# A planned order for five engines, drawn up again with other assumptions on instruction pages

## The chip, the cores and the metric

The kernel runs on one NeuronCore of one Trainium2 chip. The core has five engines with a queue of instructions each: TensorE (PE: matmuls from SBUF into PSUM), VectorE (DVE), ScalarE (ACT), GpSimd (POOL) and SyncE (SP, which here only issues transfers). Transfers run on 16 DMA engines. The metric is device time in microseconds (us) of one execution, 278.59 before (median of 3 runs, 278.31 to 279.34).

## The reference

`x` is 4 batches of 12800 rows of 128, `inducing` is 32 rows of 128. First two attention steps, then a gated layer:

```
def mab(q, kv):
    s = scale * (q @ kv.transpose(0, 2, 1))
    s = s - s.max(-1, keepdims=True)
    a = np.exp(s)
    a /= a.sum(-1, keepdims=True) + 1e-09
    return a @ kv
h = mab(I, x)                 # 32 x 128 for each batch: sums over all 12800 rows
x = mab(x, h)                 # every row attends to the 32 rows of h
gate_pre += conv_w[k][None, None, :] * xp[:, k:k + S, :]     # k = 0..4, causal
gate = 1.0 / (1.0 + np.exp(-gate_pre))
val = x @ w_val
return (gate * val @ w_out)
```

The 32 weights `a` of a row go straight into the gate and value matmuls, with `h` folded into the weights.

## The kernel before

A batch is cut into four strips of 3200 rows that lie on four groups of 32 partitions, and a strip into 7 or 8 chunks of up to 480 columns (`SIZES`). In all there are 29 chunks. Each chunk goes through these stages, whose names are those of the table `ORDER`:

- `s1`: scores of the inducing rows against the chunk (L476), copied out with their maximum by DVE (L484).
- `x` (first batch only): transposes of the chunk on PE (L451), evicted by ACT or DVE, in place of a second load.
- `gm`: maximum over a group of chunks (L497 on POOL, L505 on PE, L512 on DVE).
- `h`: exponentials (ACT, L522), transposes (DVE, L527) and the sums over the rows on PE (L542), added up by DVE (H, L552 and L554).
- `u`: normalisation of a batch's sums (ACT and POOL, then L591 and L592 on PE); `w`: gate and value weights from it (L610); `W`: their transposes on PE (L666), two halves, copied out by ACT or DVE (L676, L674); `po`: scaling of the output weights (L694).
- `s2`: second attention of a chunk: scores (L740), then a chain of softmax steps over DVE, POOL and ACT up to the tiles `P1` and `P2` (L813, L820).
- `r k`: r block k: gate matmuls of chunk k (L834) and, put in at two places of it, value matmuls of chunk k-1 (L843). ACT takes the tanh (L893), DVE multiplies (L903), ACT and POOL split the product into two halves (L916, L921).
- `o k r`: output of strip r of chunk k, three matmuls (L944 to L946; L937 for the last chunk), evicted by DVE if its number is in `OUTV`, else by ACT (L959, L961), and stored.
- `z`: fillers, matmuls on zeros (L998) that do nothing but keep PE going; eight more (L987) stand at the very start.

PE gets its work in the order of `ORDER`, word for word. For the other engines a planner, `lay`, sets the order: it keeps a clock for each engine, takes the next step whose inputs are there, and of several the one that PE needs first, where `URGE` shifts each kind of step. Its durations are constants of the source. Loads of `xt` and `xk` are issued on SP up to the first r block and on ACT from then on (`sp`, L409 and L423), in the place that the planner gives them; a load into a buffer that is still read waits at the head of its queue. Stores are issued on SP, four of the end on ACT. Eight semaphores go round among all transfers, so a transfer also waits until the last one on its semaphore has landed.

PE uses its array in three kinds of tiling: `full` (x, u, w, o, z), `strips` of 32 columns (s1, s2, gm, h, W, po) and `rows` of 32 (r). A change of kind has a price in the plan (`SWITCH`).

The plan also keeps account of PE's instructions. They come in pages of 256. The plan has a page asked for when PE is 0.68 of a page into the one before the last (`ASK`), and lets it arrive after a time that depends on the loads then under way, `bus - t`, at most `LINE`, and on `FETCH`; where PE comes to the page earlier, the plan lets it wait:

```
asked.append(t + min(max(bus - t, 0.0), LINE) + FETCH)
```

These are numbers of the plan; nothing of them is sent to the chip but the orders that come out.

Of the kernel before, what the change touches and what calls it, by code (L numbers as in the profile page):

```python
# [45 lines left out]
PAGE, ASK, NEED, LINE, FETCH = 256, 0.68, 1.8, 3.8, 2.5  # L46
# [8 lines left out]
class Plan:  # L55
# [87 lines left out]
    def lay(self, deps, succ, topo, nominal):  # L143
# [30 lines left out]
        while len(seq) < n:  # L174
# [21 lines left out]
            if e == "PE":  # L196
# [7 lines left out]
                while told > PAGE * (len(asked) + ASK):  # L204
                    t = start + (PAGE * (len(asked) + ASK) - begun) / w * work
                    asked.append(t + min(max(bus - t, 0.0), LINE) + FETCH)
# [44 lines left out]
def tile_kernel(ctx: ExitStack, tc: tile.TileContext, xt, xk, indT_in, w64, out):  # L251
# [827 lines left out]
    "tile_kernel.f_ind": 88.5,  # L1079
    "tile_kernel.f_zero": 58,  # L1080
    "tile_kernel.f_const": 124.5,
    "tile_kernel.f_mask": 39,
    "tile_kernel.warm_up": -3,
    "idle.f": 301.5,
    "load_xt.f": -120.5,
    "s1.f": -326.5,
    "s1.g": -126,
    "make_xk.ones": 310,
    "make_xk.tp": 180,
    "make_xk.ev": 114,  # L1090
    "make_xk.<lambda>": -72.5,
    "gmax.f0": 489,
    "gmax.f1": -64.5,
    "gmax.f2": 52,
    "e1.f": 26,
    "e1.tr": 172,
    "h.f": -105.5,
    "h.acc": 342.5,
    "tile_kernel.f_wload": 46.5,
    "weights.start": -12.5,  # L1100
    "weights.<lambda>": 78.5,
    "weights.cmax": 313,
    "load_xk.f": -235,
    "prep.f0": 155,
    "prep.<lambda>": -308,
    "prep.f1": -97,
    "prep.f2": 12.5,
    "prep.f3": -151.5,
    "prep.f4": 186,
    "s2.f": -222.5,  # L1110
    "s2.tin": 120.5,
    "s2.mx": 65,
    "s2.sub": -115.5,
    "s2.ex": 101.5,
    "s2.sm": -96.5,
    "s2.sa": -18.5,
    "s2.rz": 34.5,
    "s2.nm": 43.5,
    "s2.tout": 70.5,
    "s2.hi": -298,  # L1120
    "s2.lo": -152,
    "prep2.f4": 26,
    "prep2.g0": 79.5,
# [86 lines left out]
```

## Time and profile before

| | before |
|---|---|
| median of the runs, us | 278.59 (278.31 to 279.34) |
| profiled execution, us | 278.39 |
| its span, us | 276.3 |
| PE busy, us | 267.6 |
| DVE, ACT, POOL busy, us | 230.7, 197.1, 207.5 |
| moved by DMA | 75.41 MB, mean 273 GB/s |

The span is the stretch that the profiler sees; the profiled execution has 2.1 us around it. Busy time of PE counts a matmul from its start to a modelled end, and matmuls overlap in the pipeline: a PE that is busy all the time isn't at its peak, and the distance of two starts tells what one costs. The four matmuls of a group of strips or rows run beside each other, so their starts lie a few ns apart. An f32 matmul is two records, a transpose one. Where one engine waits for another, the views name the instruction that ended the wait; "issue" is time in which PE waited for nothing that the profile shows.

### The profile page before, as it was taken

To read this page: it belongs to the slowest core of one execution; us is meant where nothing else is said; L and a number is where in the kernel's file an instruction comes from. 1 tells how busy PE (TensorE), PEld (TensorE's weight loads), DVE (VectorE), ACT (ScalarE), POOL (GpSimd) and SP (SyncE) were. 2 spreads that over 40 slices of the span, in tenths; PEclk is the share of its full clock that TensorE was granted. 3 is DMA by queue.
4 is the path that set the end of the run, shared out by engine and by line. 5 is a ranking of instruction groups with operands and counts; after the bars stand their busy time and mean duration, and the time that the engine had idled before them with its cause. 6 is when DMAs were issued, how large, how long until landed. Compare 5 with 4: busy or idle time off the path is not lost.

```text
span 276.3 us, 10032 instructions
## 1 busy us (share of the span) xinstructions
PE 267.6 (97%) x4118; PEld 140.5 (51%) x4118; DVE 230.7 (83%) x542; ACT 197.1 (71%) x298; POOL 207.5 (75%) x236
## 2 busy tenths in 40 slices
PE   8999899999999999999999999999999999999983
PEld 2567546446644564475444564574444445444541
DVE  0378799999889999888889999989889998785851
ACT  2366368668848885887668778876668888787773
POOL 2000378799578999985876999998689999998650
PEclk9999999999999999999999999999999999999999
DMA  7999999997999979999949897422533125325538
GB/s 278 422 420 411 414 412 384 372 368 256 346 369 393 310 274 329 385 362 362 391 170 293 255 400 293 179 99 97 187 120 114 70 103 214 135 108 209 186 125 302
DMA packets 35373, 75.41 MB, mean 273 GB/s; under 512 B 2816, under 2 KB 26752, under 8 KB 35328
## 3 DMA queue, kind: packets, MB, share of 16 engines
q1 hardware_dynamic: 19120, 42.03, 39.7%
q10 hardware_dynamic: 16208, 32.75, 33.7%
q8 instruction: 32, 0.52, 0.8%
q14 instruction: 13, 0.11, 0.1%
HBM read 48.56 MB, written 26.21 MB: 271 GB/s over the span
## 4 chain that ended last, share of the span: by engine, by line
PE 91%; DVE 4%; ACT 2%; POOL 1%; issue 1%; POOLq 0%; ACTq 0%
PE g L834 30%; PE a L944 9%; PE a L740 8%; PE a L476 8%; PE a L946 8%; PE a L945 8%; PE a L542 7%; PE a L843 6%; PE g L998 2%; PE g L451 2%; PE a L987 1%; PE a L666 1%; DVE ss L484 1%; PE a L937 1%; DVE et L527 1%
## 5 line engine op out<-in xcount | busy, mean ns | idle before, releaser
L921 POOL TENSOR_TENSOR gl<-tg,gh 128x960 f16<-128x960 f32 (+4 forms) x56 | 104.8, 1881 | 16.1 <-PE a L946 10.2
L834 PE MATMUL g<-P,W 32*128 32x480 f16 (+4 forms) x1740 | 102.8, 345 | 0.1
L903 DVE SCALAR_TENSOR_TENSOR tg<-tg,a 128x480 f32<-128x480 f32 (+4 forms) x116 | 65.4, 604 | 10.1 <-PE a L843 8.5
L916 ACT CAST gh<-tg 128x960 f16<-128x960 f32 (+4 forms) x56 | 51.9, 929 | 29.3 <-DVE tg L903 28.8
L834 PEld LDWEIGHTS <-W 32*128 32x128 f16 x1740 | 50.6, 92 | 40.9 <-issue 10.0
L893 ACT ACTIVATE tg<-g,gsc 128x960 f32<-128x960 f32 (+4 forms) x58 | 55.5, 990 | 3.3 <-PE g L834 2.5
L843 PE MATMUL a<-P,W 32*128 32x480 f16 (+4 forms) x348 | 41.5, 344 | 0.2
L959 DVE TENSOR_SCALAR os<-a,osc 128x480 f32<-128x480 f32 (+4 forms) x62 | 40.0, 670 | 1.8 <-PE a L946 1.3
L944 PE MATMUL a<-gh,wo 128*128 128x480 f16 (+4 forms) x112 | 39.6, 354 | 0.7 <-DVE tg L903 0.7
L945 PE MATMUL a<-gh,wo 128*128 128x480 f16 (+4 forms) x112 | 39.3, 351 | 0.0
L946 PE MATMUL a<-gl,wo 128*128 128x480 f16 (+4 forms) x112 | 39.3, 351 | 0.0
L961 ACT ACTIVATE os<-a,osc 128x480 f32<-128x480 f32 (+4 forms) x46 | 28.1, 629 | 7.9 <-PE a L946 7.8
L820 POOL TENSOR_TENSOR P<-pt,P 128x480 f16<-128x480 f32 (+4 forms) x29 | 30.0, 1036 | 2.0 <-ACT P L813 1.0
L802 POOL TENSOR_TENSOR e<-e,z 128x480 f32<-128x480 f32 (+4 forms) x29 | 27.2, 938 | 4.6 <-DVE z L795 2.7
L757 POOL TENSOR_TENSOR e<-e,m 128x480 f32<-128x480 f32 (+4 forms) x29 | 27.0, 937 | 2.6 <-DVE m L751 2.2
L542 PE MATMUL a<-xk,et 128*32 128x129 f32 x800 | 27.9, 274 | 1.1 <-DVE H L554 0.6
L542 PEld LDWEIGHTS a<-xk,et 128*32 128x32 f32 x800 | 24.4, 110 | 6.5 <-issue 2.6
L740 PE MATMUL a<-xt,hT 128*32 128x480 f32 (+4 forms) x232 | 27.7, 543 | 0.0
L476 PE MATMUL a<-xt,indT 128*32 128x480 f32 (+4 forms) x232 | 26.6, 538 | 0.0
L484 DVE TENSOR_SCALAR_CACHE_REDUCE ss<-a 128x480 f32<-128x480 f32 (+4 forms) x29 | 17.3, 605 | 10.2 <-PE a L476 9.1
L763 ACT ACTIVATE e<-e 128x480 f32<-128x480 f32 (+4 forms) x29 | 16.6, 571 | 6.9 <-POOL e L757 6.7
L944 PEld LDWEIGHTS <-wo 128*128 128x128 f16 x112 | 11.2, 100 | 19.8 <-issue 10.4
(111 smaller groups left out, 322.9 us busy)
## 6 DMA issues: line engine op xcount, KB each, us to landing
out_dram<-os SPq DMA_DIRECT2D x52, 240.0 KB, 2.5
xt<-in_xt_dram ACTq DMA_DIRECT2D x11, 960.0 KB, 8.1
out_dram<-os SPq DMA_DIRECT2D x44, 224.0 KB, 3.4
xk<-in_xk_dram ACTq DMA_DIRECT2D x9, 967.5 KB, 9.1
xk<-in_xk_dram ACTq DMA_DIRECT2D x7, 903.0 KB, 7.4
xt<-in_xt_dram SPq DMA_DIRECT2D x6, 960.0 KB, 9.7
xt<-in_xt_dram ACTq DMA_DIRECT2D x5, 896.0 KB, 6.9
xk<-in_xk_dram SPq DMA_DIRECT2D x4, 903.0 KB, 12.8
```

The costliest lines, as they stand in the source:

```text
L476: T.matmul(s[32 * r:32 * r + 32, :n], c_["indT"], x[:, o:o + n // 32, r, :], start=True, stop=True)
L542: T.matmul(t[32 * s:32 * s + 32, :P + 1], st["et", b, c][:, 32 * i:32 * i + 32], st["xk", b, q][:, m + i, :], start=j < R, stop=j >= len(b ...
L740: T.matmul(s[32 * r:32 * r + 32, :n], st["hT", b], x[:, m:m + nb, r, :], start=True, stop=True)
L834: T.matmul(st[f"g{r // 2}", b, c][:, r % 2, :n], st["W", b][q, w, k, :], st[("P1", "P2")[e]][q, o:o + n], start=u == 0, stop=u == len(taps ...
L843: T.matmul(st["a", "v", b, c, r][:, :n], st["W", b][q, w, TAPS, :], st[("P1", "P2")[e]][q, o:o + n], start=u == 0, stop=u == 2)
L893: S.activation(t[:, :, :n], st[f"g{p}", b, c][:, :, :n], AF.Tanh, scale=st["gsc", b])
L903: V.scalar_tensor_tensor(t, t, 1.0, st["a", "v", b, c, r][:, :n], ALU.add, ALU.mult)
L916: S.copy(sb(pw, g1, [P, 2, CW], F16)[:, :, :n], st[tg][:, :, :n])
L921: G.tensor_tensor(sb(pw, g2, [P, 2, CW], F16)[:, :, :n], st[tg][:, :, :n], st[g1][:, :, :n], ALU.subtract)
L944: T.matmul(t, w[:, 0], st[g1][:, q, :n], start=True, stop=False)
L945: T.matmul(t, w[:, 1], st[g1][:, q, :n], start=False, stop=False)
L946: T.matmul(t, w[:, 0], st[g2][:, q, :n], start=False, stop=True)
```

## The change

Two lines of the planner's account of pages are changed, and everything that a search chooses is chosen anew under them: `ORDER` (with the places of the value matmuls in the r blocks), `URGE` and `OUTV`. The work itself is the same: the same matmuls and tiles, 24 matmuls on zeros, the same bytes in and out.

```
-PAGE, ASK, NEED, LINE, FETCH = 256, 0.68, 1.8, 3.8, 2.5
+PAGE, ASK, NEED, LINE, FETCH = 256, 0.68, 1.8, 4.0, 2.5
...
-                    asked.append(t + min(max(bus - t, 0.0), LINE) + FETCH)
+                    asked.append(t + (max(bus - t, 0.0) + 0.3 if bus - t < 0.8 and not 36.0 < t < 56.0 else LINE if t < 40.0 else LINE + 0.8) + FETCH)
...
 ORDER = [
-    ('z', 10, 2), ('z', 4, 1), ('z', 11, 2), ('s1', 0, 0), ('s1', 0, 2), ('x', 0, 2), ('x', 0, 0), ('s1', 0, 1),
...
+    ('s1', 0, 0), ('x', 0, 0), ('z', 11, 2), ('z', 4, 1), ('s1', 0, 1), ('x', 0, 1), ('s1', 0, 2), ('x', 0, 2),
...
-    "rblock.f": -517.5,
+    "rblock.f": -618,
...
-    1, 3, 4, 7, 8, 9, 11, 12, 14, 15, 20, 21, 23, 24, 25, 28, 31, 32, 34, 35, 36, 37, 39, 42, 43, 44, 45, 48, 52,
+    0, 1, 2, 3, 4, 6, 7, 11, 12, 13, 14, 20, 21, 22, 24, 25, 26, 32, 33, 34, 35, 36, 37, 38, 42, 44, 45, 49, 50, 53,
```

In the plan a page now comes 0.3 + 2.5 after the loads under way if these end within 0.8 us (and not between 36 and 56 us), else always the full 4.0 + 2.5 or, from 40 us on, 4.8 + 2.5 after it is asked for. Outside that stretch it was at most 3.8 + 2.5 and less where the loads ended sooner. `OUTV` holds 67 outputs instead of 66. Of changes of kind `ORDER` holds 116 instead of 109: 15 instead of 12 up to the first `u`, 27 instead of 21 up to `r 1`.

PE just after the eight matmuls at the start, before: two groups of fillers, then the scores of chunk 0 and of chunk 2.

```order
22 L998 MATMUL g_142<-zero 128x512
23 L998 LDWEIGHTS zero
24 L998 MATMUL g_144<-zero 128x512
25 L998 LDWEIGHTS zero
26 L998 MATMUL g_144<-zero 128x512
27 L476 MATMUL a<-xt,indT 32x128 x4
28 L476 MATMUL a<-xt,indT 32x480 x4
29 L451 MATMUL g_160<-identf,xt 128x128 x8
```

The same place of PE after (L476 32x128 is chunk 0, 32x320 chunk 1, 32x480 chunk 2; L451 are their transposes):

```order
17 L476 MATMUL a<-xt,indT 32x128 x4
18 L451 MATMUL g_144<-identf,xt 128x128 x4
19 L998 LDWEIGHTS zero
20 L998 MATMUL g_152<-zero 128x512
21 L998 LDWEIGHTS zero
22 L998 MATMUL g_152<-zero 128x512
23 L998 LDWEIGHTS zero
24 L998 MATMUL g_156<-zero 128x512
25 L476 MATMUL a<-xt,indT 32x320 x4
26 L451 MATMUL g_163<-identf,xt 128x128 x8
```

Scores and transposes of chunk 0 now stand ahead of the fillers, of which three stand here instead of five, and chunk 1 comes before chunk 2.

PE behind r block 1, before: one chunk's second scores, then the first three groups of sums of the second batch (L542, 14 instructions each), then an output.

```order
446 L834 MATMUL g_831<-P_115,W 128x320
447 L740 MATMUL a<-xt,hT 32x480 x4
448 L542 MATMUL a<-xk,et 32x129 x42
449 L944 LDWEIGHTS wo
450 L944 MATMUL a<-gh,wo 128x128
451 L945 LDWEIGHTS wo
452 L945 MATMUL a<-gh,wo 128x128
```

The same place of PE after:

```order
449 L834 MATMUL g_830<-P_115,W 128x320
450 L542 MATMUL a<-xk,et 32x129 x14
451 L740 MATMUL a<-xt,hT 32x480 x4
452 L542 MATMUL a<-xk,et 32x129 x14
453 L476 MATMUL a<-xt,indT 32x448 x4
454 L834 LDWEIGHTS W
455 L834 MATMUL g_1000<-P_115,W 128x480
```

The second scores have moved between the first two groups of sums, the third group has left the place, and the first scores of a chunk of the second batch (L476) stand in front of r block 2.

ACT around the two copies of the first batch's weights (L676), before:

```order
28 L676 COPY W<-a 128x768
29 L813 CAST P_115<-pt 128x160
30 L676 COPY W<-a 128x768
31 L763 ACTIVATE e<-e 128x480
32 L409 DMA xt<-in_xt_dram 128x4x480
33 L893 ACTIVATE tg<-g_707,gsc 128x2x128
34 L893 ACTIVATE tg<-g_710,gsc 128x2x128
35 L409 DMA xt<-in_xt_dram 128x4x448
```

The same place of ACT after (L409 loads a chunk, L893 is the tanh of r block 0):

```order
28 L676 COPY W<-a 128x768
29 L813 CAST P_115<-pt 128x160
30 L763 ACTIVATE e<-e 128x480
31 L409 DMA xt<-in_xt_dram 128x4x448
32 L676 COPY W<-a 128x768
33 L813 CAST P_115<-pt 128x320
34 L409 DMA xt<-in_xt_dram 128x4x480
35 L712 ACTIVATE wof<-w,uv 128x128
36 L893 ACTIVATE tg<-g_726,gsc 128x2x128
```

The first load on ACT is now issued ahead of the second copy and is another chunk's, and the second load is issued ahead of the tanh of r block 0 instead of behind it.

## Rows read from the trace of the kernel before

**Rows 1.** The page, part 1: busy us, share of the span, instructions.

```profile
PE 267.6 (97%) x4118; PEld 140.5 (51%) x4118; DVE 230.7 (83%) x542; ACT 197.1 (71%) x298; POOL 207.5 (75%) x236
```

**Rows 2.** Windows, the middle: length, busy us of each engine (instructions), clock, DMA share, GB/s.

```profile
50.00:262.00 212.00, 212.00 (x3309) 108.29 (x3311) 190.86 (x422) 161.91 (x238) 185.81 (x184) 1.00 0.70 250
```

**Rows 3.** Waits of PE: who waited for whom, us in total, times, longest.

```profile
PE a L987 <- DVE warm L278: 1.2, 1, 1.2
PE a L591 <- POOL H L585: 0.7, 1, 0.7
PE a L944 <- DVE tg L903: 0.7, 1, 0.7
PE a L542 <- DVE H L554: 0.6, 1, 0.6
PE a L542 <- DVE et L527: 0.5, 1, 0.5
PE g L451 <- ACT xk L456: 0.3, 1, 0.3
```

**Rows 4.** Timeline of PE, start: start us, us, instruction, count.

```profile
4.56 2.53 PE L998 MATMUL g<-zero 128*128 128x512 f16 x5
7.02 1.23 PE L476 MATMUL a<-xt,indT 128*32 128x128 f32 x16
...
10.38 0.65 PE L451 MATMUL g<-identf,xt 128*128 128x128 f32 x4 [0.34 <-ACT xk L456]
...
26.84 2.51 PE L542 MATMUL a<-xk,et 128*32 128x129 f32 x79
```

**Rows 5.** DMA issues: count, KB each, median us from issue to landing.

```profile
xt<-in_xt_dram SPq DMA_DIRECT2D x1, 320.0 KB, 3.1
```

**Rows 6.** Timeline of PE, fillers behind the first batch's normalisation.

```profile
31.39 1.24 PE L998 MATMUL g<-zero 128*128 128x512 f16 x4
```

**Rows 7.** The chain that ended last, 40 to 52 us: start us, us, what.

```profile
43.34 0.16 issue
...
48.44 0.30 DVE H L554
48.74 0.24 issue
```

**Rows 8.** Windows, between the two stops of PE.

```profile
43.49:48.95 5.46, 4.90 (x127) 3.77 (x126) 5.46 (x15) 4.87 (x10) 3.64 (x4) 1.00 1.06 374
```

**Rows 9.** The page, part 3: a DMA queue, its kind, packets, MB, share.

```profile
q8 instruction: 32, 0.52, 0.8%
```

**Rows 10.** The page, part 5: the second scores, busy us and mean ns.

```profile
L740 PE MATMUL a<-xt,hT 128*32 128x480 f32 (+4 forms) x232 | 27.7, 543 | 0.0
```

**Rows 11.** Timeline of ACT: a load's issue, and the third batch's second weights copy.

```profile
103.76 1.84 ACTq L409 DMA_DIRECT2D xt<-in_xt_dram  x1
164.55 0.80 ACT L676 COPY W<-a 128x768 f16<-128x768 f16 x1 [0.15 <-PE a L666]
```

**Rows 12.** Timeline of PE, from an output to an r block.

```profile
252.15 0.37 PE L945 MATMUL a<-gh,wo 128*128 128x480 f16 x1
252.35 0.37 PE L946 MATMUL a<-gl,wo 128*128 128x480 f16 x1
252.65 0.58 PE L834 MATMUL g<-P,W 32*128 32x480 f16 x8
```

**Rows 13.** Timeline of PE, the third batch's weights and r block 15.

```profile
163.81 0.69 PE L666 MATMUL a<-ident,w 128*32 128x128 f16 x24
...
166.24 1.89 PE L834 MATMUL g<-P,W 32*128 32x448 f16 x36
```

**Rows 14.** Windows, the end.

```profile
268.00:270.00 2.00, 2.00 (x12) 0.95 (x11) 1.25 (x2) 0.85 (x3) 1.50 (x1) 1.00 1.02 377
...
272.00:274.00 2.00, 0.13 (x1) 0.00 (x0) 0.00 (x0) 0.69 (x2) 0.00 (x0) 1.00 1.00 368
```

**Rows 15.** Timeline of SP, the last store.

```profile
272.75 0.38 SPq L968 DMA_DIRECT2D out_dram<-tg  x1
```

More of the change, by code (lines that the diff above doesn't have):

```diff
@@ L1078 @@
 URGE = {
[L1079 to L1120, printed above, removed]
@@ L1121 @@
-    "s2.lo": -152,
-    "prep2.f4": 26,
-    "prep2.g0": 79.5,
-    "prep2.g1": -255.5,
-    "prep2.<lambda>": -134,
-    "prep2.g2": 21.5,
-    "prep2.g3": -43.5,
-    "prep2.f8": -194.5,
-    "prep3.f6": -252.5,
-    "prep3.f7": -52,
-    "rblock.f": -517.5,
-    "rblock.th": -130.5,
-    "prep_out.f0": -46.5,
-    "prep_out.f1": -28.5,
-    "prep_out.f2": -104,
-    "prep_out.f3": 189.5,
-    "prep_out.<lambda>": -271.5,
-    "prep_out.f4": -102.5,
-    "rblock.gv": -277,
-    "halves.hi": 53.5,
@@ L1141 @@
-    "halves.lo": 269.5,
-    "outp.f": 135.5,
-    "outp.ev": -307.5,
-    "outp.store": -219.5,
+    "tile_kernel.f_ind": 51.5,
+    "tile_kernel.f_zero": 31,
+    "tile_kernel.f_const": 13,
+    "tile_kernel.f_mask": 95.5,
+    "tile_kernel.warm_up": -117,
+    "idle.f": 352.5,
+    "load_xt.f": -80.5,
+    "s1.f": -341.5,
+    "s1.g": -171.5,
+    "make_xk.ones": 311,
+    "make_xk.tp": 10.5,
+    "make_xk.ev": 54,
+    "make_xk.<lambda>": -174,
+    "gmax.f0": 508.5,
+    "gmax.f1": -173,
+    "gmax.f2": 47,
@@ new lines @@
+    "e1.f": 7.5,
+    "e1.tr": 83,
+    "h.f": -127.5,
+    "h.acc": 232,
+    "tile_kernel.f_wload": 63,
+    "weights.start": -58.5,
+    "weights.<lambda>": 2,
+    "weights.cmax": 197,
+    "load_xk.f": -256,
+    "prep.f0": 212,
+    "prep.<lambda>": -271,
+    "prep.f1": -84.5,
+    "prep.f2": -31,
+    "prep.f3": -134.5,
+    "prep.f4": 83.5,
+    "s2.f": -191,
+    "s2.tin": 228,
+    "s2.mx": 72,
+    "s2.sub": -51.5,
+    "s2.ex": 44.5,
+    "s2.sm": -104.5,
+    "s2.sa": -96.5,
+    "s2.rz": 54,
@@ new lines @@
+    "s2.nm": 22.5,
+    "s2.tout": 188.5,
+    "s2.hi": -291.5,
+    "s2.lo": -127.5,
+    "prep2.f4": -162.5,
+    "prep2.g0": 142.5,
+    "prep2.g1": -261,
+    "prep2.<lambda>": -99.5,
+    "prep2.g2": -33,
+    "prep2.g3": -108.5,
+    "prep2.f8": -296,
+    "prep3.f6": -178.5,
+    "prep3.f7": -34.5,
+    "rblock.f": -618,
+    "rblock.th": -107.5,
+    "prep_out.f0": -197.5,
+    "prep_out.f1": -23,
+    "prep_out.f2": -157.5,
+    "prep_out.f3": 155,
+    "prep_out.<lambda>": -290.5,
+    "prep_out.f4": -75,
@@ L1145 @@
+    "rblock.gv": -261,
+    "halves.hi": 134,
+    "halves.lo": 318.5,
+    "outp.f": 196.5,
+    "outp.ev": -312.5,
+    "outp.store": -161,
 }
```

79 rows, old and new, of tables (ORDER, OUTV) are left out of this document.

## Prediction

> **What bounds the kernel now.** I read the page's first part first: TensorE (PE) is busy 267.6 us of the span, the next engine, VectorE (DVE), 230.7 [rows 1]. Then one window over the long middle: from 50 to 262 us PE is busy in all 212.00 us, while the DMA engines are busy 70% of it [rows 2]. So in four fifths of the span only PE's own work counts, and that work is the same before and after: both orders hold 4118 matmul records, 24 of them fillers on zeros. A new order can change the time in five ways: what PE waits for, what the fillers cost where they stand, how often PE changes its kind of tiling, what happens after its last matmul, and new waits.
>
> The list of PE's waits is short [rows 3]: 1.2 us for the first tile of zeros, which nothing in the change touches, and five others of 0.7, 0.7, 0.6, 0.5 and 0.3 us, together 2.8 us. That is the whole stock from which a gain can come, and one of them (0.7 us, the outputs' first matmul after the last value block, which waits until DVE has freed a PSUM bank) stays, because the last two r blocks are still followed by an output and have the same neighbours. 2.1 us are left. The profiled execution took 278.39 us, its span 276.3 and 2.1 around it; the median of the runs is 278.59, 0.2 above. Sums below start from 278.39.
>
> **The start, to the first batch's normalisation (0 to 31 us).** Before, the eight warm-up matmuls are followed by five fillers that take 2.53 us, about 0.50 each, and real work starts at 7.02 [rows 4]. After, the scores of chunk 0 (s1 0 0) and its four transposes (x 0 0) stand there instead, then three fillers; the other two come later. The load that they need is the first in the queue and lands 3.1 us after its issue at 0.7 [rows 5], before 4.56, so nothing waits. What is pulled ahead is worth, by its rows, 128 of the 608 columns of the 1.23 us group, 0.26, and at most 0.65 for the transposes [rows 4], of which some 0.15 is the last one's tail: 0.5; together 0.76 us. At this place a filler takes 0.50 against 0.31 later (1.24 us for four, [rows 6]), so I take double for real work too: 1.5 us, and 1.3 to 1.5 for three fillers and two changes of kind at 0.1 (below): the next scores begin at 4.56 + 1.5 + 1.5 = 7.56, 0.54 later than real work did before, with 0.76 done: -0.2 us. The two fillers that come later cost 0.3 each, +0.6. Up to the normalisation there are 15 changes of kind instead of 12, +0.3. Against that, the waits for the xk copy (0.3) and for the transposed sums (0.5) [rows 3] stand where a filler or another chunk's scores now stand; neither is sure to go, I take half, -0.4. Sum: +0.3 us. Bounds: -0.5 if both waits go and the fillers fill what would have been waited, +1.1 if none goes and the chunk that now loads last (7) makes a wait like the 0.5 again.
>
> **From there to the sums of the second batch (31 to 50 us).** PE has the same matmuls up to the first value block in both orders; the ten fillers stay, r block 0 stands after the output scaling's matmul and one more chunk of scores, where its weights' copy has more time. Two stretches here are not work: the chain has PE at "issue" for 0.16 us at 43.34 and for 0.24 us at 48.74, the second one behind the wait for DVE's sum of H that ends at 48.74 [rows 7]. Between the two stops, from 43.49 to 48.95, lie 127 matmuls and 126 weight loads [rows 8], with the few waits of PE's own about 256 instructions; and one DMA queue of kind "instruction" carried 32 packets of 0.52 MB in all, 16 KB each [rows 9], which is 4118 matmuls and as many loads of 64 bytes. I read the two stops as PE out of instructions: at equal distances, the next page not there. Both orders pass the second boundary after the same 728 matmuls. What changes is what stands there: before it is the third group of sums, which also waits for H; after, one group has been put behind r block 2, and the scores of chunk 4 stand at the boundary. So the wait for H (0.36 of the 0.6) goes if the page does not come last anyway. By my reading the page was last, at 48.74 + 0.24 = 48.98 [rows 7]: what goes in front of it is given back at the page. So the stop moves with the time at which the page is asked for. I place that a little over a page earlier, just ahead of r block 1 (an estimate: no row shows the asking). There, before, PE is in the small matmuls of the maxima with both chunks of scores behind it; after, half a chunk of scores is still to come, some 0.4 us by the mean of its group (27.7 us for 29 chunks, 0.96 each, [rows 10]), so the page is asked for 0.3 sooner. I take -0.3 us, with -0.8 (all of 0.16, 0.24 and 0.36) and +0.3 (a page that comes as late and less work in front of it) as ends.
>
> The Trainium skill's Runtime: NRT & Kernel Launch, Instruction fetch mechanics, says that an engine's sequencer fetches the next block of 256 instructions on a DMA queue of its own while it works on this one, and that the cost of crossing a block is mostly hidden. The size agrees with the packets of [rows 9]; the hiding does not agree with the two "issue" pieces of [rows 7] while the DMA engines are busy all the time (1.06 in [rows 8]). By that rule both stops would be plain waits for other engines, this part would give -0.8 instead of -0.3, and the sum below would be 278.0.
>
> **The loads on ScalarE's queue (ACT).** The first load for batch 1's second half now stands ahead of the copy of the weights' second half (L676) and fetches the chunk that is needed first. A load's issue takes about 0.4 us of ACT's queue, but one in a burst held it 1.84 us [rows 11]. There were ten pairs and a triple of adjacent loads, now eight pairs and a triple. I cost this at 0: between the transposes and r block 0 now stand two fillers (0.62, [rows 6]) and a chunk of scores (0.96, [rows 10]), the copy takes 0.80 [rows 11], and 0.8 us of cover are left. What it costs if a load is held is the third rival.
>
> **The middle (50 to 262 us).** No wait to win. A change of kind costs 0.1: L945 and L946 start 0.20 apart, L946 and the r block 0.30 [rows 12]. From r block 1 on there are 89 in the new table instead of 88: +0.1 us. New waits: the shortest distance that shrinks is r block 15, which needs the second half of the third batch's weights. Before, three outputs stood between its transposes, which ended at 163.81 + 0.69 = 164.50, and the block at 166.24 [rows 13], 0.58 each; the copy ran from 164.55 to 165.35 [rows 11], 0.89 ahead of the block. Now two outputs stand there and 0.3 us are left: 0, with +0.3 if the eviction that now stands ahead of the copy runs over.
>
> **The end (262 to 276 us).** The last stores fill the DMA engines: 377 GB/s at 268 to 270, and still 368 at 272 to 274, when PE is done [rows 14]. Eleven stores (nine chunks of 240 KB and two of 352) leave after the last value block in both, 2.9 MB, about 7.9 us at this rate, so the end hangs on the first of them, which ACT evicts behind the same cast. That the last one is now 240 KB instead of the 352 issued at 272.75 [rows 15] only reorders them: 0, ends -0.4 and +0.3.
>
> **Sum.** +0.3 - 0.3 + 0 + 0.1 + 0 = +0.1: 278.5 us.
>
> **Rivals.** (1) The stock is won: the waits for xk, for the transposed sums, for the POOL sum of H (0.7) and for H all go, 2.1 us, and the 0.16 of the first stop, 2.3; with the 0.2 pulled ahead and less 0.9 for fillers and kinds that is 278.39 - 1.6 = 276.8. For it: each of these waits is at a place whose order is new. Against: the 0.7 follows from the last sums of batch 0, whose last 82 matmul records stand in the same order as before, and the ten fillers that mark the same waits are all still there. (2) The stops were no pages: 278.0, as above; still no change by the measure below. (3) ACT's loads hold its queue where PE waits for ACT: ahead of the copy for r block 0 (0.8 us of cover) and two loads ahead of that for r block 15 (0.3). Held 1.84 instead of 0.4 like the one of [rows 11], the first would cost 1.44 - 0.8 = 0.6 and the second 1.44 - 0.3 = 1.1: 278.5 + 1.7 = 280.2; a hold begins to cost from 0.7 us on, and it decides from about 1.8. For it: the hold has been seen, with DMA just as full. Against: at r block 15 two loads stood as near before and did not hold, and there are fewer bursts. (4) The change does nothing to the stops: its rule on pages only moves a plan; then +0.4, 278.8.
>
> **How the numbers follow.** About 0.5% (1.4 us) can be told from no change: faster is below 277.2, slower above 280.0. My forecast together with (2) and (4), which differ from it by less than that, gets 0.62; (1) 0.18; (3) and other new waits of its size in a middle that now has none 0.20. The bounds of the terms, in quadrature, give -1.0 and +1.1 around 278.5; taking in half of (1) and most of (3) the range is 277.0 to 280.5. The forecast's own is 277.6 to 279.6.
>
> **What would show it.** Right: PE without a wait from 52 to 262 us, real work from about 4.6 us and the second scores at 7.4 to 7.7, 82 sums starting at 26.9 to 27.5 (26.84 before, [rows 4]), a stop without an engine to blame near 43.5 and near 49, the last store's start and the end within 0.4 us of before's. Wrong: a PE wait for ACT's L676 before r block 0 or 15 (rival 3), no stop at 49 (rival 2), PE past the normalisation before 30.5 us (rival 1).

## The result, and the profile after

The changed kernel takes 281.28 us (median of 6 runs, 280.44 to 282.41) against 278.45 for the kernel before beside it (278.08 to 279.34): 1.0098 times, 95% interval 1.0078 to 1.0117. It is 2.8 us slower; 278.5 was predicted, and the range ended at 280.5. The profiled execution took 282.41, its span 280.6, the longest of the six. The figures of the run sw34 below leave out one execution of 310.29 us, at a granted clock of 0.85, which the 280.0 of later expectations still counts.

The page's first part, as [rows 1]: PE is busy 1.8 us longer for the same 4118 matmul records.

```profile
PE 269.4 (96%) x4118; PEld 140.5 (50%) x4118; DVE 231.0 (82%) x543; ACT 197.1 (70%) x297; POOL 207.4 (74%) x236
```

The window over the middle, as [rows 2]: 1.66 us are missing from PE's 212.

```profile
50.00:262.00 212.00, 210.34 (x3264) 106.59 (x3257) 187.44 (x416) 159.79 (x234) 181.64 (x180) 1.00 0.70 246
```

PE's waits, as [rows 3]: the three of 0.6, 0.5 and 0.3 us have gone, and four have come.

```profile
PE a L476 <- DMA xt<-in_xt_dram: 1.2, 2, 1.0
PE a L987 <- DVE warm L278: 1.2, 1, 1.2
PE a L476 <- DVE H L554: 1.0, 1, 1.0
PE a L542 <- issue: 0.8, 1, 0.8
PE g L834 <- POOL P L820: 0.8, 1, 0.8
PE a L591 <- POOL H L585: 0.8, 1, 0.8
PE a L944 <- DVE tg L903: 0.7, 1, 0.7
```

The timeline of PE (start, us, instruction, count, in brackets the idle time before it and what ended it) shows where they stand. The first six lines answer to [rows 4]; then come the stop near 48 us, r blocks 3 and 4, the stop near 70, one near 112 that the list above does not name (eight matmuls of scores, 1.01 us at 13.96, take 1.68), and the first output behind the last value block.

```profile
4.70 0.66 PE L476 MATMUL a<-xt,indT 128*32 128x128 f32 x8
...
6.07 1.03 PE L998 MATMUL g<-zero 128*128 128x512 f16 x3
7.03 0.75 PE L476 MATMUL a<-xt,indT 128*32 128x320 f32 x8
...
13.96 1.01 PE L476 MATMUL a<-xt,indT 128*32 128x480 f32 x8 [1.03 <-DMA xt<-in_xt_dram]
...
27.12 0.87 PE L542 MATMUL a<-xk,et 128*32 128x129 f32 x24
...
47.39 1.23 PE L542 MATMUL a<-xk,et 128*32 128x129 f32 x28
49.65 0.58 PE L476 MATMUL a<-xt,indT 128*32 128x448 f32 x4 [1.02 <-DVE H L554]
...
58.09 0.38 PE L834 MATMUL g<-P,W 32*128 32x480 f16 x4
59.28 0.39 PE L834 MATMUL g<-P,W 32*128 32x480 f16 x4 [0.81 <-POOL P L820]
...
65.55 0.38 PE L834 MATMUL g<-P,W 32*128 32x480 f16 x2
...
69.31 1.62 PE L542 MATMUL a<-xk,et 128*32 128x129 f32 x47
71.77 0.49 PE L542 MATMUL a<-xk,et 128*32 128x129 f32 x9 [0.84 <-issue]
...
112.84 1.68 PE L476 MATMUL a<-xt,indT 128*32 128x480 f32 x8
...
268.16 0.36 PE L944 MATMUL a<-gh,wo 128*128 128x480 f16 x1 [0.69 <-DVE tg L903]
```

Two kinds of cause are left to tell apart. At r block 3 PE waits for a semaphore of POOL. At the other three places it stands at a fixed distance in its own instruction stream: counted in the records of matmuls, weight loads and waits, the stops follow the 1472nd, the 2240th and about the 3519th, each 192 (or 191) more than a multiple of 256; the two stops of the kernel before [rows 7] follow the 1216th and the 1472nd. Each time PE goes on 1.1 to 1.6 us after one 16 KB packet of the instruction queue [rows 9] has ended. The DMA view of 0.1 us at 69.4 holds the packet for the stop at 70.7; the kernel before had this page at 63.7, 5.4 us before it was needed.

```profile
q8 instruction: 1, 0.02, 62.1%
```

When a page is asked for stands in no view, so the asking is an estimate here. There are 32 packets for some 8300 records, one for every 256, and in none of the 13 profiles of the table below does one begin before 161 of its 256 records are through; where DMA is idle, most begin soon after that. The asking is put at the 165th, 283 records ahead of the place of the stop.

### The profile page after: what moved, and what is told of

It is laid out like the page before. It is cut to its first block, busy times and chain, and to the rows that moved or that the text cites. A ratio compares the mean times of both kernels' runs of the same rounds, so it can differ in the third digit from the quotient of the medians.

```text
span 280.6 us, 10031 instructions
## 1 busy us (share of the span) xinstructions
PE 269.4 (96%) x4118; PEld 140.5 (50%) x4118; DVE 231.0 (82%) x543; ACT 197.1 (70%) x297; POOL 207.4 (74%) x236
## 3 DMA queue, kind: packets, MB, share of 16 engines
HBM read 48.56 MB, written 26.21 MB: 266 GB/s over the span
## 4 chain that ended last, share of the span: by engine, by line
PE 83%; DVE 5%; DMA 4%; ACT 2%; issue 2%; POOL 1%; SPq 1%; ACTq 0%
PE g L834 29%; PE a L944 9%; PE a L945 7%; PE a L946 7%; PE a L740 7%; PE a L542 7%; PE a L476 7%; PE a L843 6%; DMA xt<-in_xt_dram 4%; PE a L666 1%; PE g L451 1%; ACT xk L456 1%; PE a L937 1%; DVE et L527 1%; DVE e L746 1%
## 5 line engine op out<-in xcount | busy, mean ns | idle before, releaser
L921 POOL TENSOR_TENSOR gl<-tg,gh 128x960 f16<-128x960 f32 (+4 forms) x56 | 104.7, 1880 | 13.8 <-PE a L946 8.0
L893 ACT ACTIVATE tg<-g,gsc 128x960 f32<-128x960 f32 (+4 forms) x58 | 55.5, 992 | 4.9 <-PE g L834 4.9
L959 DVE TENSOR_SCALAR os<-a,osc 128x480 f32<-128x480 f32 (+3 forms) x63 | 39.6, 655 | 2.6 <-PE a L946 2.3
L961 ACT ACTIVATE os<-a,osc 128x480 f32<-128x480 f32 (+3 forms) x45 | 27.8, 638 | 5.5 <-PE a L946 5.4
L802 POOL TENSOR_TENSOR e<-e,z 128x480 f32<-128x480 f32 (+4 forms) x29 | 27.1, 939 | 5.6 <-DVE z L795 3.5
L476 PE MATMUL a<-xt,indT 128*32 128x480 f32 (+4 forms) x232 | 28.1, 545 | 2.2 <-DMA xt<-in_xt_dram 1.2
L542 PE MATMUL a<-xk,et 128*32 128x129 f32 x800 | 29.1, 275 | 0.9 <-issue 0.8
L542 PEld LDWEIGHTS a<-xk,et 128*32 128x32 f32 x800 | 24.9, 110 | 7.8 <-issue 3.5
L813 ACT CAST P<-pt 128x480 f16<-128x480 f32 (+4 forms) x29 | 16.3, 562 | 8.3 <-DVE pt L808 8.2
```

What stands on the lines that cost most here:

```text
L476: T.matmul(s[32 * r:32 * r + 32, :n], c_["indT"], x[:, o:o + n // 32, r, :], start=True, stop=True)
L542: T.matmul(t[32 * s:32 * s + 32, :P + 1], st["et", b, c][:, 32 * i:32 * i + 32], st["xk", b, q][:, m + i, :], start=j < R, stop=j >= len(b ...
L893: S.activation(t[:, :, :n], st[f"g{p}", b, c][:, :, :n], AF.Tanh, scale=st["gsc", b])
L921: G.tensor_tensor(sb(pw, g2, [P, 2, CW], F16)[:, :, :n], st[tg][:, :, :n], st[g1][:, :, :n], ALU.subtract)
```

## The experiments

Theory S, named so in the expectations: the loss is a sum of separate stops (the wait at r block 3, and pages that come late because loads stand in front of them). Its rival R: the loss is spread (changes of kind, engines that lag). The table has what the traces of all profiles show. A stop is the time from one matmul's start to the next across it, where 0.1 to 0.2 is normal; near 112 it is the same, without the 0.3 to 0.4 us by which the four strips run unevenly behind it.

| profile | r block 1 starts | stop near 48, its end | at r block 3 | near 70 | near 112 | span |
|---|---|---|---|---|---|---|
| before | 42.65 | 0.87, 48.99 | - | - | - | 276.3 |
| before_again | 42.76 | 0.85, 49.08 | - | - | - | 276.6 |
| after | 43.07 | 1.30, 49.65 | 1.19 | 1.12 | 0.40 | 280.6 |
| again | 41.62 | 1.66, 48.56 | 1.19 | - | - | 277.4 |
| hold7 | 42.17 | 1.60, 49.05 | 1.18 | - | 0.94 | 279.2 |
| rule_b | 41.81 | 1.78, 48.88 | 2.47 | - | 0.73 | 282.4 |
| hold12 | 41.74 | 1.67, 48.71 | 1.19 | 1.59 | - | 282.7 |
| sw34_again | 41.67 | 1.68, 48.65 | - | - | - | 277.3 |
| fix | 41.93 | 1.78, 49.24 | - | - | - | 279.4 |
| sw_h47 | 42.04 | 0.50, 47.83 | - | - | - | 276.5 |
| headA | 41.55 | 1.72, 48.74 | - | - | - | 276.2 |
| headA_h4 | 41.91 | - | - | - | - | 275.2 |
| before_h4 | 41.83 | - | - | - | - | 274.9 |

**The two kernels again (again, before_again).** No edit.

> The changed kernel once more, unaltered, for a second profile. Theory S (separate stops of TensorE make up the loss): median 281.3 as before; the wait for POOL's P in front of r block 3 (0.9 us at 58.1) comes again at the same place, because it follows from the order, while the stops where the instruction packet is late (48.4, 70.7 and 112.9 us in the first profile: 1.0, 0.8 and 0.7) stand at the same instructions but vary by some tenths from run to run, and a run that is 1 us shorter than the first profile has 1 us less of them. Theory R (the loss is spread: eight more changes of kind and engines that lag, and the stops are taken out of slack): 281.3 too, but stops elsewhere or none, and the r blocks 4, 5 and 9 come no later against the kernel before than in proportion to the work done.

280.94 us (4 runs, 279.19 to 282.38), 1.0097 times before, interval 1.0060 to 1.0134. The wait at r block 3 is there again, to the hundredth. The stops near 70 and 112 are not, and the execution is 3.2 us shorter than the one first profiled. The order of the matmuls is the same, so the two can be set side by side: the first profile is 1.44 us later behind the scores of chunk 3 (their load is waited for 1.03, here 0.35, and the first matmuls run slower), 1.09 behind the stop near 48, and loses 1.18 more near 70, 0.42 near 112 and 0.49 in the sums near 120.

> The kernel before once more, for a second profile. Theory S: page packets near 64 and 104 us start within 1.8 us of the asking again, no stop behind 52 us, r block 1 within 0.4 us of 42.65. Rival (the start and the pages vary as much in the kernel before, and its first profile was a lucky one): stops behind 52 us, or r block 1 off by a microsecond.

278.66 us, starts and stops within 0.11 of the first profile, the span within 0.3: in its two profiles the kernel before has no such places behind 52 us. Two other executions of it on record took 281.58 and 281.67, and no profile shows why.

**Chunk 3's softmax in front of chunk 4's (sw34, sw34_again).**

```diff
-    ('z', 14, 2), ('s1', 1, 3), ('W', 0, 1), ('z', 13, 2), ('po', 0), ('s2', 0, 4), ('r', 0), ('gm', 1, 0),
-    ('s2', 0, 3), ('r', 1, 0, 6), ...
+    ('z', 14, 2), ('s1', 1, 3), ('W', 0, 1), ('z', 13, 2), ('po', 0), ('s2', 0, 3), ('r', 0), ('gm', 1, 0),
+    ('s2', 0, 4), ('r', 1, 0, 6), ...
```

> In the changed kernel the softmax of chunk 3 (s2 0 3) and that of chunk 4 (s2 0 4) change places, so that chunk 3 comes first as in the kernel before. Theory S: r block 3 no longer waits for POOL's P (L820): 0.9 us less, 281.3 - 0.9 = 280.4, between 279.9 and 280.9. Theory R (VectorE and POOL are behind as a whole here, so that the order of two chunks only moves the wait): 281.3, and a wait of about the same size shows up at r block 4 or at the outputs after it.

279.87 us (9 runs), 1.0037 times before, interval 1.0008 to 1.0066: 1.07 less than the 280.94 of the changed kernel beside it, where Theory S expected 0.9.

> The kernel of the run sw34 once more, for an undisturbed profile. Theory S: r block 3 starts without a wait for POOL's P, r block 4 follows it 6.4 to 6.5 us later instead of 7.45, and what is left against the kernel before are the stops for pages near 48, 70 and 112 us, in sum 0 to 2 us. Rival R: a wait of 0.5 us or more between r blocks 3 and 5 that is no page.

279.10 us in one run, 279.15 for before beside it. The timeline has r block 3 and r block 4 6.46 us apart, where the first profile has 7.46 (58.09 and 65.55), and no wait:

```profile
57.09 0.58 PE L834 MATMUL g<-P,W 32*128 32x480 f16 x8
...
63.55 0.38 PE L834 MATMUL g<-P,W 32*128 32x480 f16 x2
```

So the swap is worth 1.0 us at this place. Not all of it reaches the end. Against the run again, whose matmuls stand in the same order but for a few, this execution is 0.89 us ahead from r block 3 on; 0.42 is lost at the outputs behind r block 4, where PE now waits for an eviction of ACT, and some 0.4 more near 110 and 118 us, so that the spans differ by 0.1 (277.3 and 277.4).

```profile
73.10 0.36 PE L944 MATMUL a<-gh,wo 128*128 128x480 f16 x1 [0.27 <-ACT os L961]
```

That is Theory R in part. By the medians the swap is worth 1.07, by these two profiles, each the shortest of its kernel, 0.1; how much of the 1.07 is the wait itself is not shown.

The chain that ended last in the changed kernel says how: the maximum of batch 1's scores is masked on POOL (L497) ahead of chunk 3's normalisation (L802), and that on POOL waits for VectorE, which waits for scores that PE has just finished.

```profile
54.45 1.79 PE a L476 x16
...
56.85 0.09 DVE ss L484
56.94 0.07 issue
57.01 0.21 POOL m L497
57.22 0.81 POOL e L802
58.04 0.09 issue
58.13 1.11 POOL P L820
59.24 0.04 issue
59.28 0.39 PE g L834 x4
```

In the kernel before the same subtraction on POOL began at 55.79 and was done 0.35 us ahead of r block 3 (57.24). There was no slack for a chunk that comes one place later.

```profile
55.79 1.10 POOL L820 TENSOR_TENSOR P<-pt,P 128x480 f16<-128x480 f32 x1
```

**The changed tables under the old planner lines (rule_b).**

```diff
-PAGE, ASK, NEED, LINE, FETCH = 256, 0.68, 1.8, 4.0, 2.5
+PAGE, ASK, NEED, LINE, FETCH = 256, 0.68, 1.8, 3.8, 2.5
-                    asked.append(t + (max(bus - t, 0.0) + 0.3 if bus - t < 0.8 and not 36.0 < t < 56.0 else LINE if t < 40.0 else LINE + 0.8) + FETCH)
+                    asked.append(t + min(max(bus - t, 0.0), LINE) + FETCH)
```

> The changed kernel's tables (order, urgencies, places of loads and outputs) under the kernel before's two planner lines on pages. Theory S: the loss lies in the order table; the lines only shift a few instructions of the other engines, 281.3 within 0.5, with the wait at r block 3 as it was. Rival (the new rule on pages put loads and copies where they make the page stops): 279 to 279.5, with the stops at 70.7 and 112.9 us gone.

283.79 us (4 runs), 1.0163 times before (1.0112 to 1.0215). Both missed: the lines are not what costs, and without them it is worse by more than the 0.5 allowed. In this order POOL splits a product for the outputs (L921, 1.39 us) ahead of chunk 3's P, and the wait at r block 3 grows from 1.19 to 2.47, as the chain that ended last shows:

```profile
57.40 1.39 POOL gl L921
58.79 1.06 POOL P L820
59.84 0.04 issue
59.89 0.39 PE g L834 x4
```

That is 1.3 of the difference in this profile; r block 4 comes 1.7 later still, because PE's granted clock falls after this stop. Of the four executions the one whose granted clock was 1.00 as a mean took 281.15, the three others 283.4 to 284.3. Windows of 1 us (columns as in [rows 2]) have it at 0.50, the level of 1.2 GHz, from 61 to 64 us, and at 1.00 from 65 on:

```profile
58.00:59.00 1.00, 0.00 (x0) 0.00 (x0) 0.35 (x2) 0.59 (x1) 1.00 (x2) 1.00 1.09 396
...
61.00:62.00 1.00, 1.00 (x16) 0.41 (x11) 1.00 (x2) 0.00 (x0) 0.00 (x0) 0.50 0.97 361
...
65.00:66.00 1.00, 1.00 (x16) 0.65 (x13) 0.25 (x1) 0.77 (x1) 0.36 (x1) 1.00 0.00 0
```

**Loads behind the asking, near 64 us (hold7).** The planner gets an earliest time for single operations, by their numbers; these are three loads.

```diff
-        n = len(ops)
+        n = len([ops[i].update(early=t) for i, t in HOLD.items()]) * 0 + len(ops)
-BW = 424e3
+BW, HOLD = 424e3, {423: 69.0, 438: 67.9, 442: 67.9}
```

> In the changed kernel three loads for batch 2 (two of xt, one of xk) are put 6 to 8 instructions later on ScalarE's queue, so that they are issued after the time at which, by the distance in instructions, the page for 70.7 us should be asked for (about 64.3). Nothing else is moved on TensorE. Theory S, with the page fetched behind the loads that were issued before it: its packet starts 2 to 3 us earlier, the stop at 70.7 (0.8 to 1.1 us) goes, 281.3 - 0.9 = 280.4; if the later loads make the scores of batch 2 wait, up to 0.5 of it comes back. Rival (the stop at 70.7 is no page, or the page waits for the outputs' stores and not for these loads): the stop stays, 281.3, or 281.8 with the scores' wait.

280.87 us (6 runs), 1.0074 (1.0051 to 1.0097). The packet moved as expected: 64.8 here, 66.3 in the run again, 69.4 in the first profile, and the sums that were cut at 70.7 run through. From the estimated asking it is 1.2 us here, and 1.1 and 1.2 in fix and sw_h47, which hold the same loads back; in the five profiles of this order that do not, it is 3.1 to 5.7. The stores on record around that time stay where they were, so they are not what held the page up.

```profile
68.70 2.72 PE L542 MATMUL a<-xk,et 128*32 128x129 f32 x85
```

The time followed only by some tenths (0.07 against the run again, 0.41 against the first six): this stop was not in every execution to begin with, 0.4 us came back as a wait in front of the scores of batch 2, and the stop near 112 was larger in this one.

**One load behind the asking near 106 us (hold12), and swap and loads together (fix).** HOLD is {771: 109.5}; fix has the swap and {423: 68.0, 438: 66.9, 442: 66.9, 771: 108.3}.

> In the changed kernel one load (xt of batch 3, first chunk) is put seven instructions later on ScalarE's queue, behind the time at which the page needed near 112 us should be asked for (about 106). Two loads of xk stay in front. Theory S, with the page behind the loads issued before it: its packet starts about 2 us earlier after the asking (3 instead of 5.2 us), the stop at 112 us (0.65 us with its tail in the first profile, more in two others) goes, and the page after it is no longer late either: 281.1 - 0.6 = 280.5. Rival (the lateness does not come from these loads): stop and time stay, 281.1; if the load that is now the third makes the sums of batch 2 wait near 121 us, up to 0.4 of the gain is lost.

283.12 us (4 runs), 1.0154 (1.0132 to 1.0176): 2 us slower instead of faster. Neither theory had that. The stop near 112 is gone, but the run again has none either, and the packet came 4.1 us after the estimated asking in both, so for this page nothing is shown. The planner moved other work with the load, and PE now stands 1.44 us at 129.7, waiting for VectorE's tg, and then runs r block 11 at the lower clock, 1.3 longer. The lower clock is not what makes the median: two executions with a granted clock of 1.00 as a mean took 283.29 and 282.95. The profiled execution also has the stop near 70 at its longest. The experiment changed more than its cause.

```profile
131.10 0.31 PE L944 MATMUL a<-gh,wo 128*128 128x352 f16 x1 [1.17 <-DVE tg L903]
```

```profile
133.00:134.00 1.00, 1.00 (x10) 0.30 (x12) 0.93 (x4) 0.76 (x2) 1.00 (x1) 0.50 1.06 412
```

> The changed kernel with chunk 3's softmax in front of chunk 4's again, and with the loads that stood in front of two askings for pages put behind them (three loads near 64 us, one near 106). Theory S: the wait at r block 3 (0.9) and the two stops (0.4 and 0.5 as a mean over the profiles) go and at most 0.6 comes back as waits for later loads: 279.3 to 279.9. What is left against the kernel before is the page near 48 us, eight changes of kind and 0.3 at the end. Rival (stops are only moved): 280.0 to 280.4, no better than the swap alone (280.0).

281.03 us (6 runs), 1.0094 (1.0073 to 1.0116): outside both expectations, and 1.2 slower than the swap alone. Its profile has hold12's wait for tg (1.44 again), without the lower clock, and none of the stops at r block 3, 70 and 112. That wait stands in the two profiles in which the load near 106 is moved, and in no other.

**The start alone, on the kernel before (headA).** Its order up to ('u', 0) is the changed kernel's, the rest its own.

> The kernel before, with the changed kernel's order of TensorE and of the first loads up to the first batch's normalisation (u 0); everything behind it, the urgencies and the planner's lines stay those of before. Theory S: the new start is not where the 2.7 us are lost. In four profiles of kernels that hold it r block 1 began 0.4 later in one and 0.5 to 1.0 us earlier in three than in the profile of before, and a part of it is given back at the page that is late near 48 us: 278.2, between 277.6 and 278.7. Rival (seven more changes of kind and the late load of chunk 3 are paid in full): 279.2 or more.

278.72 us (11 runs), 1.0007 (0.9993 to 1.0022): neither the gain of 0.3 expected nor the rival's loss. In this profile r block 1 starts 1.1 us earlier than in the first profile of before, and the stop near 48 takes 0.85 of it back: it ends at 48.74, 0.25 earlier than before. But the start of the kernel before varies by nearly as much. In before_h4 below, whose first 40 us hold the same matmuls in the same order, the five fillers of [rows 4] take 1.71 us instead of 2.53, and r block 1 starts at 41.83 instead of 42.65:

```profile
4.56 1.71 PE L998 MATMUL g<-zero 128*128 128x512 f16 x5
6.20 1.23 PE L476 MATMUL a<-xt,indT 128*32 128x128 f32 x16
```

Against that profile the new start is 0.3 us faster here and 0.1 slower in headA_h4, so no gain of the start is shown.

```profile
45.36 1.93 PE L542 MATMUL a<-xk,et 128*32 128x129 f32 x56
48.74 1.07 PE L542 MATMUL a<-xk,et 128*32 128x129 f32 x28 [1.45 <-DVE m L751]
```

**One load behind the asking near 41 us (headA_h4, before_h4, sw_h47).** HOLD is {307: 42.4} on headA, {307: 42.6} on the kernel before, and {300: 42.4, 423: 68.0, 438: 66.9, 442: 66.9} with the swap on the changed kernel.

> The kernel before with the same load put behind the asking (about 42.5). Theory S: the packet starts near 44 instead of 46.5, the stop at 48.1 ends with the wait for H at 48.75 instead of the page at 48.99: 278.4, between 278.1 and 278.6, so hardly faster, but the packet must move. Rival (the page does not wait for this load): packet at 46.5, stop of 0.87 us as before, 278.6.

277.75 us (12 runs), 0.9975 (0.9953 to 0.9998), 0.9 less and more than expected, though the interval all but reaches 1: six executions took 276.8 to 277.4, six 278.1 to 279.3, and the profiled one (276.98) is of the first six. What the others paid is not shown. In the kernel before, a load of batch 1 left at 40.75, ahead of the asking, and the next at 43.32; now both leave together:

```profile
42.42 1.13 ACTq L409 DMA_DIRECT2D xt<-in_xt_dram  x2
```

The page's packet, which came at 46.53 before, is in the DMA view of 0.1 us at 43.7:

```profile
q8 instruction: 1, 0.02, 98.4%
```

And the three chunks' sums, cut for 0.87 us before, run without a stop:

```profile
45.75 2.70 PE L542 MATMUL a<-xk,et 128*32 128x129 f32 x80
48.38 0.23 PE L944 MATMUL a<-gh,wo 128*128 128x128 f16 x1
```

From r block 1 to r block 2 it is 6.83 us instead of 7.62; the profiled execution is shorter by another 0.82 for its start alone. So the whole stop was the page. The wait for VectorE's H that the list of waits names there [rows 3] was not the last to end: here the third group of sums starts at 47.29, ahead of that H (L554), which starts at 47.62.

> The kernel before with the changed kernel's start (as in the run headA, 278.7 us, whose profile gained 1.1 us up to r block 1 and lost 0.85 of it at the stop near 47 us), and with one load (xt of batch 1, chunk 4) put four instructions later on ScalarE's queue, behind the asking for the page needed there (about 41.4); the next load follows it. Theory S: the page's packet, which started at 46.1, starts about 2.3 us earlier, the stop of 1.4 us shrinks to the wait for VectorE's sum of H, and the gain of the start is kept: 277.8, between 277.3 and 278.2. Rival (VectorE sets the end of that stop, or the page does not wait for this load): 278.7, stop unchanged. Second rival (the later load is waited for by the scores of chunk 4 of batch 1): 279.

277.53 us (12 runs), 0.9963 (0.9944 to 0.9981): faster than both kernels, and the packet starts at 43.66 instead of 46.05. From r block 1 to r block 2 it is 6.83 us here too, instead of 8.47 in headA.

> The changed kernel with chunk 3's softmax in front of chunk 4's, one load behind the asking near 41 us, and three behind the asking near 64 us. Theory S: against 280.0 for the swap alone, 0.5 less at the page near 48 and 0.4 less on average at the page near 70, 0.3 back for a later H: 279.4, between 279.0 and 279.9. What is left is the page near 112 us, changes of kind and the end. Rival: 280.0 or more.

279.07 us (10 runs), 1.0017 (0.9992 to 1.0043): with the swap and the loads behind the askings the changed order can't be told from before. Its stop near 48 is 0.50 (the packet moved less than in the two runs above: 4.3 us after the estimated asking, against 4.8 to 5.6), and of the others none is left in the profile. Against before_h4, which has the same page mended on the old order, it is 1.3 us slower: 0.4 of that is the rest of the stop near 48, 0.4 a new wait in front of the scores near 73, and what remains is not told apart.

## Why the prediction was wrong

**The middle is the step that failed.** It was costed at +0.1 with "no new waits", and "the shortest distance that shrinks is r block 15". That distance held (no wait for L676), but it was not the shortest: r block 3 needs chunk 3's P, whose s2 item the change had put behind chunk 4's. The row of POOL at 55.79 against 57.24 would have given 0.35 us of slack against a full chunk of POOL's and VectorE's work. Measured: starts 1.18 to 1.19 us apart across the wait in four profiles that have the order and 2.47 in rule_b, where 0.2 is normal; 1.07 less in the median when the two items change places (sw34), of which some may be other waits.

**Pages were followed at one boundary only.** The prediction read the stops as missing pages, rightly, and then looked at the second alone, though [rows 9] has 32. At 70.7 and 112.9 the change put a load ahead of the estimated asking (63.12 against 64.27, 105.78 against 105.98) where the next one stood behind it before (64.14 against 62.87, 102.76 against 102.12). The late pages cost 1.12 and 0.40 (0.65 with the strips behind it) in the profile of 282.41, nothing in that of 279.19; holding loads back (sw_h47) takes the swap's 1.0037 to 1.0017, with intervals that overlap. That the stop near 70 is a page is shown by its place and packet, and that these loads delay it by hold7; for the one near 112 only the place and packet are shown, no intervention.

**The page near 48 (predicted -0.3, "asked 0.3 sooner").** The mechanism was right, the size was not, and in the first profile not the sign. By the distance in records the page is asked for at 42.15 instead of 42.49 (an estimate from those records), as predicted, but its packet started at 46.97 instead of 46.53: it is served behind the loads issued before it. The stop ended 0.66 later in the first profile and 0.43 earlier in the second. The wait for H (0.36), which the lower end of -0.8 still counts as a gain, was none (before_h4).

**The start (predicted +0.3).** The 82 sums began 0.28 later in the first profile (27.12 against 26.84), the second scores at 7.03, ahead of the 7.4 to 7.7 expected, and chunk 3's scores waited 1.03 for their load: the upper bound's "chunk that now loads last" was in mind, chunk 3, fifth in the queue, was the one. Over the eight profiles of the changed order r block 1 starts at 42.0 as a mean (41.62 to 43.07), over three with the old start at 42.4 (41.83 to 42.76): a difference inside the spread. In the times the new start makes 0.0 (headA against before) and -0.2 (headA_h4 against before_h4), both within the noise, so the +0.3 is neither confirmed nor refuted. The sum took 0.50 us as the price of a filler at this place; that was the price in one execution, 0.34 in another of the same order.

**Loads on ACT, changes of kind, the end.** No r block waited for ACT's weights copy: 0, as costed, and rival 3's mechanism fell, though its sign and size (280.2) were nearest. Of changes of kind there are 117 instead of 109 in the order, eight and not the four that were costed: the sum left out the stretch between the first `u` and r block 1, and the one between the warm-up matmuls and the first scores. At 0.1 each [rows 12] that is 0.4 more, which no run separates. From the first output behind the last value block to the end of the span it is 12.44 us (268.16 to 280.6) instead of 12.16, +0.28, inside the bounds of -0.4 and +0.3.

**The rivals.** The stock of (1) was indeed won in part (xk, et), but inside the start. Rival (2), by which the stops were no pages, is refuted by before_h4. Rival (4) is answered in part by rule_b: with the new tables the planner's lines do move work, by 2.8 us (283.79 against 280.94 on the same chip, with intervals that overlap a little and one of four executions at 281.15), and for the better; what they do with the old tables no run shows. The rule of the Trainium skill's Runtime: NRT & Kernel Launch, Instruction fetch mechanics, that crossing a block is mostly hidden, holds in these traces for most of the 32 pages and fails where loads are queued in front (0.87 us in the kernel before).

**The sum.** The new wait at r block 3 (1.07 by the medians), pages between 0 and about 2 us from one execution to the next, 0.3 at the end in the first profile and the changes of kind make up the 2.8. Only the first is shown as a share of the median. How the rest divides is not settled, since each execution has its own pages, and the 1.3 us between sw_h47 and before_h4 say that part of the loss is spread, as the rival R had it.

## What to carry to other kernels

After a reordering, list every consumer whose producer's item moved behind another of its kind, and take its slack from the engine that finishes last, not from the engine that waits. Where TensorE runs without waits and DMA is full, its instruction pages are loads with a deadline: find the boundaries by counting instructions, and issue no data load just ahead of an asking; behind it, the same load let the page through (before_h4, hold7). Check what else the planner moves with the load: in hold12 and fix that cost more than the page. A stop that a profile blames on a semaphore may be a page; a faster start that is given back at a fixed instruction is a sign of it. Before a gain of some tenths is read from one profile, profile the unchanged kernel more than once: here its start alone varied by 0.8.

## What the runs showed of the hardware

An instruction page is served behind data loads issued earlier, and this can be steered: one load put four instructions later on its queue moved the packet by 2.8 us (46.53 to 43.77; from 4.0 to 2.1 us after the estimated asking) and took a stop of 0.87 us away. While the DMA engines were full, packets began up to 8.0 us after the estimated asking; while they were nearly idle (a share under 0.2), 39 of 41 began within 1.1. At the stops PE went on 1.1 to 1.6 us after the packet's end; the packet itself took 0.9 to 1.1 there.

The same program at a granted clock of 1.00 in its middle took 3.2 us more or less (spans 277.4 and 280.6): two pages were late in one execution and in time in the other, and 1.1 us came from the start. A stop can cost more than its length: after 2.47 us (rule_b) and after 1.44 us (hold12) the granted clock was 0.50 for some 3.4 us, 1.7 and 1.3 us lost; after another of 1.44 (fix) and those of 1.1 to 1.8 it stayed at 1.00. What decides that is not shown.
